# Eight routed experts after masked attention: one more expert fetched in quarter rows, and some low parts made by an adding transfer

## The chip, the cores and the metric

The kernel runs on one core of a Trainium2 chip. The metric is the device time of one execution in microseconds; runs are summed up by their median. Engines are named as the profile names them: PE multiplies matrices (PEld loads its weights), DVE is the vector engine, ACT the scalar engine, POOL is GpSimd, SP issues transfers.

## The reference

For 8 batches of 8 heads, 576 positions and 64 columns, attention scores without a softmax are multiplied by a decay `gamma ** (i - j)` under a causal mask, and by `v`. The result, laid out as 4608 tokens of 512 columns, goes to 8 experts. Routing is greedy and exact: all token and expert scores are sorted, each token goes to the best expert that still has room, and each expert takes 576 tokens.

```
logits = x @ w_gate
order = np.argsort(-logits.flatten())
...
h = np.maximum(x[mask] @ w1[e], 0.0)      # 576 x 512 by 512 x 1024
out[mask] = h @ w2[e]                     # 576 x 1024 by 1024 x 512
```

## The kernel before

**The stages.** Attention runs first, and routing is prepared beside it. Then the eight experts follow one another, in an order that routing finds while the kernel runs. They are numbered 0 to 7 here, so "the fifth expert" is number 4 and "the sixth" is number 5. Each has a first half (`l1`, products `ph`, line 1200: hidden values of 8 blocks of 128 units for two groups of token columns, s = 0 with 256 tokens and s = 1 with 320) and a second half (`l2`, products `py`, line 1348: five tiles of tokens). Numbers 6 and 7 (from `FAST` on) have another first half, `l1_fast`, line 1278.

**High and low parts.** Each float32 operand is split in two: a high part rounded for PE, and a low part, which is the value less its high part. Each product is then three matmuls: high by high, high by low, low by high. Weights arrive in the buffers `raw`; ACT makes the high part, and the low part comes either from a DVE subtraction or from a negated ACT copy of `raw` and a transfer that adds `raw` to it (`conv_lo`, line 1007, issued on POOL). The latter gives the rounded value with the opposite sign plus the value, which is the same difference. For second-half weights of experts 1, 2 and 3 the adding transfer is issued in two halves.

**Token rows.** An expert's rows are gathered from the scratch tensor `xd` by indirect transfers issued on POOL. Below `QUART` (which is 5 before) they come as whole rows: five transfers (line 1065), four PE transposes for each of five tiles (line 1154), an ACT copy for the high part (line 1156), a DVE subtraction for the low part (line 1157). From `QUART` on they come as quarter rows: 18 transfers (line 1076), a DVE transpose of 32 by 32 blocks for each of five tiles (line 1136), an ACT copy (line 1138), a DVE subtraction (line 1129), with PE taking no part. In the first half of the expert before, a quarter transfer waits behind a small POOL copy of a fresh hidden value (line 1075). The transposed rows are `xh` and `xl`. The s = 0 products read tiles 0 and 1, the s = 1 products tiles 2, 3 and 4.

**Routing beside the experts.** For the experts to come, a generator (`phases`) issues search rounds (line 351 on PE, chains of short DVE instructions around it), `members` (lines 421 and 422 on PE), `listing` (lines 459 and 462 on PE, then lines 495, 496 and 469 to 480 on DVE, which write the indices for the gathers), `leave` (lines 505 to 516) and `best` (lines 209 to 221).

**The order of instructions** is the order in which the program issues them, on each engine by itself. Where a routing step stands among the matmuls is set by a planner, `Mixer`, which adds up assumed durations in ns: `t` for PE, `v` for DVE. `adv(ns)` adds to `t` after each group of matmuls (650 for the three matmuls of one of a tile's eight blocks in `l2`, 430 in the last, smaller tile; 320 or 400 per three matmuls in `l1`). `vec(ns)` adds DVE work to `v`. When `t` reaches the time at which the planner thinks DVE is done (`v` + 150), the generator's next step is issued at that place, and its own matmuls' time is added to `t`. From expert 2 on, the DVE durations of routing are multiplied by 1.13. A tile of quarter rows is transposed at the first place where `t` has reached the due time of its last gather, 13000 after its issue; or, in the first two steps of `l1`, by force. Gathers are issued at least 1200 apart on `t`. The scatter of the results goes out on POOL, and in some experts late ones are put off to the next `l1` (`behindhand`).

At the end of `l2` the last tile `py` is moved out by an ACT copy (line 1371) and a DVE addition (line 1372). The tile's `next(tr, None)`, which issues the next piece of the following expert's transposes, stands before these two in the program; a piece that is left over is issued at the head of the following `l1`, behind them.

Of the kernel before, what the change touches and what calls it, by code (L numbers as in the profile page):

```python
# [11 lines left out]
F32 = mybir.dt.float32  # L12
F32R = mybir.dt.float32r
BF16 = mybir.dt.bfloat16
I32 = mybir.dt.int32
ALU = mybir.AluOpType
AF = mybir.ActivationFunctionType
# [3 lines left out]
NP, HP, NB = 4, 4, 9  # L21
N, DM, E, FF = 4608, 512, 8, 1024
SLACK = 1.0
QUART = 5
FAST = 6

CST = HP * 18 + 128 + 64
# [62 lines left out]
class Route:  # L90
# [337 lines left out]
    def listing(s, p):  # L428
# [45 lines left out]
        s.rows = s.idx  # L474
        if p >= QUART:
            s.rows = pool.tile([128, 20], I32, name="quart", bufs=2)
# [458 lines left out]
def moe(tc, nc, P, R, xd, w1_d, w1q_d, w2_d, out, mix):  # L935
    V, A, T = nc.vector, nc.scalar, nc.tensor
# [4 lines left out]
    state = dict(dma=0, conv=0, most=2, listing=-1, force=False)  # L941
    RAW, W1, W2, XH, XL, OPS, FEED = {}, {}, {}, {}, {}, {}, {}
# [36 lines left out]
    def free(i):  # L979
        freed.add(i)  # L980
        dma_pump()
# [16 lines left out]
    def conv_lo(by=None):  # L998

        at, raw, hi, lo = begun.pop(0)  # L1000
        e, k = divmod(at, 8)
        if by is not None:
            by.tensor_tensor(lo, raw, hi.bitcast(F32), op=ALU.subtract)
        else:
            A.activation(lo, raw, AF.Copy, scale=-1.0)
            for c in (slice(0, 512), slice(512, 1024)) if 0 < e < 4 and k >= 4 else (slice(0, 1024),):
                nc.gpsimd.dma_start(lo[:, c], raw[:, c], accum_op=ALU.add)  # L1007
        (W1 if k < 4 else W2)[e, k % 4] = (hi, lo)
        free(at)

# [45 lines left out]
    def gather(e, all=False, behind=None):  # L1056
        if e == E or not ready(e):
            return
        if e not in XG:
            xg = P["c"].tile([128, 20, 128], F32, name="xg", tag="xg")  # L1060
            XG[e] = xg
            if e < QUART:
                for j in range(5):
                    n = 128 if j < 4 else 64
                    nc.gpsimd.indirect_dma_start(out=xg[:n, 4*j:4*j+4, :].rearrange("p a c -> p (a c)"), out_offset=None, in_=xd[:, :],  # L1065
                                                 in_offset=bass.IndirectOffsetOnAxis(ap=found[e][:n, j:j+1], axis=0))
                state['arrives'] = mix.t + (9700 if e == 3 else 9000)
            else:
                LEFT[e] = list(range(18))
                state['arrives'], state['next'], state['at'] = 0, 0, {}  # L1070
        left = LEFT.get(e)
        while left and (all or mix.t >= state['next']):
            g = left.pop(0)
            if behind is not None:
                nc.gpsimd.tensor_copy(spacer4, behind.bitcast(F32))
            nc.gpsimd.indirect_dma_start(out=XG[e][:, g, :], out_offset=None, in_=xq,  # L1076
                                         in_offset=bass.IndirectOffsetOnAxis(ap=lines[e][:, g:g+1], axis=0))
            state['next'] = mix.t + 1200
            state['at'][g] = mix.t + (6000 if e >= FAST else 13000)
# [38 lines left out]
    def transposes(e):  # L1118

        if e >= FAST:  # L1120
            yield from fast_transposes(e)
            return
        xg = XG[e]
        xh = P['s'].tile([128, 4, 576], F32R, name="xh", bufs=1)
        xl = P['s'].tile([128, 4, 576], F32R, name="xl", bufs=1)
        XH[e], XL[e] = xh, xl
        if e >= QUART:
            xt = P['s'].tile([128, 4, 576], F32, name="xt", bufs=1)
            low = lambda c: V.tensor_tensor(xl[:, :, c], xt[:, :, c], xh[:, :, c].bitcast(F32), op=ALU.subtract)
            last = None  # L1130
            for j in range(5):
                n = 4 if j < 4 else 2
                while not state['force'] and state['at'].get(4*j + n - 1, mix.t + 1) > mix.t:
                    yield
                c = slice(128*j, 128*j + 32*n)
                V.transpose(xt[:, :, c].rearrange("p h (g i) -> p h g i", i=32),
                            xg[:, 4*j:4*j+n].rearrange("p g (h i) -> p h g i", h=4))
                A.activation(xh[:, :, c], xt[:, :, c], AF.Copy)
                if last is not None:
                    low(last)  # L1140
                    mix.vec(1360)
                else:
                    mix.vec(680)
                last = c
                yield
            low(last)
            mix.vec(400)
            yield
            return
        for j in range(5):  # L1150
            n = 128 if j < 4 else 64
            pt = P['bank'](("t", "h0", "h1", "h0", "h1")[j] if e else ("t", "y", "y", "t", "y")[j], [128, 4, 128], "pt", F32R)
            for d in range(4):
                T.transpose(pt[:, d, :n], xg[:n, 4*j + d].bitcast(F32R), P['ident_r'][:n, :n])  # L1154
            o, l = [x[:, :, j*128:j*128+n] for x in (xh, xl)]
            A.activation(o, pt[:, :, :n].bitcast(F32), AF.Copy)  # L1156
            V.tensor_tensor(l, pt[:, :, :n].bitcast(F32), o.bitcast(F32), op=ALU.subtract)
            mix.vec(610)
            yield
# [3 lines left out]
    def l1(e, tr):  # L1163

        hb = P['w'].tile([128, 8, 1152], F32R, name="hb", bufs=1)
        order = [(f, s) for f in (range(8) if e < QUART else (0, 4, 1, 5, 2, 6, 3, 7)) for s in range(2)]
        lows = []

        def low(ps, f, s):
            for a, b in ((0, 256),) if s == 0 else ((0, 256), (256, 320)):  # L1170
                to = (640 if a == 0 else 64) + 256*s
                V.scalar_tensor_tensor(hb[:, f, to+a:to+b], ps[:, a:b], 0.0, hb[:, f, 256*s+a:256*s+b].bitcast(F32),  # L1172
                                       op0=ALU.max, op1=ALU.subtract)
        if e == 0:
            order[1:3] = order[2], order[1]
        for i, (f, s) in enumerate(order):
            state['force'] = i < 2
            k, b = (f // 2, f % 2) if e < QUART else (f % 4, f // 4)
            wh, wl = [w.rearrange("p (f d m) -> p f d m", f=2, d=4)[:, b] for w in W1[e, k]]
            if i == 0 and e:  # L1180
                next(tr, None)
                next(tr, None)
            elif i == 1:
                for _ in tr:
                    pass
                if e == 0:
                    nc.sync.dma_start(spacer3, W1[0, 1][1][0:1, 0:1].bitcast(F32))
                    state['most'] = 8*E
                    dma_pump()
            xh, xl = XH[e], XL[e]  # L1190
            c, n = ((slice(0, 256), 256), (slice(256, 576), 320))[s]

            ps = P['bank']("y" if i // 2 in (2, 5) else f"h{s}", [128, n], "ph")
            terms = [(w[:, d], x[:, d, c]) for d in range(4) for w, x in ((wh, xh), (wh, xl), (wl, xh))]
            if (e == 0 and f < 2) or (0 < e < QUART and i == 1):
                terms = terms[0::3] + terms[2::3] + terms[1::3]
            elif e == 0 and f == 4:
                terms = terms[0::3] + terms[1::3] + terms[2::3]
            for k, (w, x) in enumerate(terms):
                T.matmul(ps, w, x, start=(k == 0), stop=(k == 11))  # L1200
                if k % 3 == 2:
                    mix.adv(320 + 80*s)
                    if e + 1 < QUART:
                        gather(e + 1)
                if k == 5 and i and e + 1 >= QUART:
                    if i % 4 != 3:
                        gather(e + 1, behind=last)
                    elif i == 7 and behindhand:
                        behindhand.pop(0)()
            A.activation(hb[:, f, c], ps, AF.Relu)  # L1210
            last = hb[0:1, f, c][:, 0:1]
            lows.append((ps, f, s))
            if i:
                low(*lows.pop(0))
            mix.vec(340 + 140*s)
            if e == 0 and i == 6:
                conv_hi()
            elif e == 0 and i == 7:
                conv_lo(V)
                mix.vec(1000)  # L1220
            if i in (2, 7, 9, 11, 13) if e == 0 else s and i // 2 in (1, 2, 3, 4):
                conv()
        owed.append(lambda: low(*lows.pop(0)))
        while behindhand:
            behindhand.pop(0)()
        return hb
# [278 lines left out]
```

## Time and profile before

| | us |
|---|---|
| median of 3 runs (605.62 to 606.1) | 605.64 |
| the profiled execution's own time | 605.43 |
| its span, first to last instruction | 603.6 |
| PE busy | 590.7 (98%) |
| DVE busy | 476.1 (79%) |
| ACT busy | 298.0 (49%) |
| POOL busy | 191.0 (32%) |

The profiled execution took 605.43 us, 1.8 more than its span, for what lies around the first and the last instruction. Matmuls are pipelined, so a busy PE is not PE at its peak; what counts is whether one matmul starts as soon as the one before allows. From the first expert on, at 160.1 us, the first halves of experts 0 to 5 take 26 to 29 us each and the second halves 25 to 31.

### The profile page before, as it was taken

The page shows a single profiled execution, that of the slowest core. Times are in us where ns is not written, and L with a number is a line of the kernel's source. Part 1 is how long each engine was busy: PE and PEld are TensorE (multiplying, and loading weights), DVE is VectorE, ACT ScalarE, POOL GpSimd, SP SyncE. Part 2 cuts the span into 40 slices and gives each one's busy share as a digit, 9 for nine tenths or more (in the row PEclk, how much of TensorE's full clock was granted, in tenths as well). Part 3 has the DMA queues.
Part 4 walks back from the last instruction along what each step waited for, and adds up shares of the span by engine and source line. Part 5 has one row for each costly group of instructions (what it writes and reads, how often), then busy time and mean ns, then how long its engine had stood idle before and what let it go on. Part 6 is the DMA issues. An engine that isn't in the chain of part 4 may idle for free.

```text
span 603.6 us, 14953 instructions
## 1 busy us (share of the span) xinstructions
PE 590.7 (98%) x5663; PEld 503.5 (83%) x5667; DVE 476.1 (79%) x1679; ACT 298.0 (49%) x649; POOL 191.0 (32%) x259
## 2 busy tenths in 40 slices
PE   9999999998999999999999999999999999999995
PEld 5887878775698889878977998799889889988973
DVE  3788989898799878987896897799985597888800
ACT  4555555542364447443662356154527357557610
POOL 0000000000511354251642362257646724861021
PEclk9999999999999999999999999999999999999998
DMA  9999999924467699795889299839876724843410
GB/s 327 401 376 334 393 351 399 351 74 150 144 194 157 206 236 243 206 228 174 184 236 257 59 226 232 233 64 241 210 207 148 211 92 107 254 147 88 114 43 35
DMA packets 51503, 125.74 MB, mean 208 GB/s; under 512 B 6352, under 2 KB 20304, under 8 KB 51432
## 3 DMA queue, kind: packets, MB, share of 16 engines
q1 hardware_dynamic: 35812, 79.77, 37.8%
q0 software_dynamic: 15296, 44.58, 32.9%
q8 instruction: 44, 0.72, 0.5%
q10 hardware_dynamic: 324, 0.45, 0.2%
q14 instruction: 27, 0.22, 0.1%
HBM read 80.21 MB, written 18.87 MB: 164 GB/s over the span
## 4 chain that ended last, share of the span: by engine, by line
PE 80%; DVE 8%; issue 6%; DMA 3%; ACT 1%; POOL 1%; POOLq 0%; SPq 0%; DVEq 0%; ACTq 0%
PE py L1348 29%; PE ph L1200 20%; PE pA L601 6%; PE pX L645 5%; PE ph L1278 4%; PE pS L624 3%; PE pX L636 2%; DMA xg<-xd,idx 2%; PE pT L683 2%; PE r L351 1%; PE warm L1443 1%; PE pt L1154 1%; DVE hb L1172 1%; PE pT L697 1%; PE r L459 1%
## 5 line engine op out<-in xcount | busy, mean ns | idle before, releaser
L1348 PE MATMUL py<-w2h,hb 128*128 128x512 f32 x576 | 186.7, 396 | 0.0
L1348 PE MATMUL py<-w2l,hb 128*128 128x512 f32 (+1 forms) x320 | 125.1, 391 | 0.0
L1348 PEld LDWEIGHTS py<-w2h,hb 128*128 128x128 f32 x576 | 104.8, 188 | 22.0
L1200 PE MATMUL ph<-xh,w1h 128*128 128x256 f32 (+1 forms) x384 | 111.2, 302 | 0.2 <-ACT xh L1156 0.2
L1200 PE MATMUL ph<-xh,w1l 128*128 128x256 f32 (+1 forms) x384 | 108.9, 296 | 0.0
L1200 PE MATMUL ph<-xl,w1h 128*128 128x256 f32 (+1 forms) x384 | 108.6, 296 | 0.0
L1065 POOL DMA_INDIRECT xg<-xd,idx x25 | 25.5, 1019 | 184.6 <-DMA raw<-in_w 152.2
L1210 ACT ACTIVATE hb<-ph 128x256 fp32r<-128x256 f32 (+1 forms) x96 | 39.1, 408 | 77.1 <-PE ph L1200 75.0
L1322 POOL DMA_INDIRECT out_y<-yt,idx x40 | 42.2, 1056 | 95.6 <-ACT yt L1369 77.2
L1200 PEld LDWEIGHTS ph<-xh,w1h 128*128 128x128 f32 x384 | 71.0, 189 | 1.3 <-ACT xh L1156 0.7
L1200 PEld LDWEIGHTS ph<-xl,w1h 128*128 128x128 f32 x384 | 71.3, 190 | 0.2
L1200 PEld LDWEIGHTS ph<-xh,w1l 128*128 128x128 f32 x384 | 71.2, 189 | 0.0
L1348 PEld LDWEIGHTS py<-w2l,hb 128*128 128x128 f32 (+1 forms) x320 | 56.7, 177 | 12.9
L1076 POOL DMA_INDIRECT xg<-xd,quart x54 | 55.4, 1026 | 15.6 <-issue 13.1
L1007 POOL DMA_DIRECT2D w2l<-raw x40 | 36.9, 1108 | 59.8 <-ACT hb L1210 47.8
L1369 ACT ACTIVATE yt<-py 128x512 f32<-128x512 f32 x32 | 19.0, 593 | 65.6 <-PE py L1348 51.3
L1172 DVE SCALAR_TENSOR_TENSOR hb<-ph,hb 128x256 fp32r<-128x256 f32 (+1 forms) x144 | 42.5, 349 | 9.7 <-ACT hb L1210 9.1
L585 ACT ACTIVATE vin<-vin,cst 128x128 f32<-128x128 f32 (+1 forms) x160 | 48.1, 379 | 1.7 <-DMA cst<-in_cst 1.7
L603 DVE TENSOR_TENSOR am<-pA,cst 128x1024 f32<-128x1024 f32 x32 | 38.9, 1214 | 12.4 <-PE pA L601 12.1
L1278 PE MATMUL ph<-xh,op 128*128 128x288 f32 x224 | 46.3, 298 | 0.2
L626 ACT ACTIVATE S<-pS 128x128 f32<-128x128 f32 x64 | 17.8, 277 | 46.0 <-PE pS L624 45.9
L601 PEld LDWEIGHTS pA<-qin,kin 64*128 64x128 f32 x512 | 31.9, 191 | 9.1 <-issue 2.9
(215 smaller groups left out, 1119.8 us busy)
## 6 DMA issues: line engine op xcount, KB each, us to landing
raw<-in_w SPq DMA_DIRECT2D x52, 512.0 KB, 5.2
w1l<-raw POOLq DMA_DIRECT2D x21, 512.0 KB, 6.9
w2l<-raw POOLq DMA_DIRECT2D x16, 512.0 KB, 5.9
kin<-in_qk SPq DMA_DIRECT2D x14, 576.0 KB, 8.0
qin<-in_qk SPq DMA_DIRECT2D x14, 576.0 KB, 6.4
vin<-in_vk SPq DMA_DIRECT2D x14, 576.0 KB, 7.7
nin<-in_vk SPq DMA_DIRECT2D x14, 512.0 KB, 8.1
xd<-xr SPq DMA_DIRECT2D x36, 192.0 KB, 6.8
```

The lines of the kernel that those rows point to most:

```text
L585: nc.scalar.activation(x, x, AF.Copy, scale=vs[:, u % HP, 4*c+h:4*c+h+1])
L601: nc.tensor.matmul(pa[:, r, j], LD[u, 'k'][half(r), s], LD[u, 'q'][half(r), s], start=True, stop=True, skip_group_check=True)
L603: nc.vector.tensor_tensor(AM[u, hf], pa, m1[:, None, None, :].to_broadcast([128, 2, 4, 128]), op=ALU.mult)
L645: nc.tensor.matmul(PX[u, hf][half(h), b, 128*c:128*c+128], v[:, a:a+64], AM[u, hf][:, h ^ b, j], start=False, stop=False, skip_group_check ...
L1007: nc.gpsimd.dma_start(lo[:, c], raw[:, c], accum_op=ALU.add)
L1076: nc.gpsimd.indirect_dma_start(out=XG[e][:, g, :], out_offset=None, in_=xq, in_offset=bass.IndirectOffsetOnAxis(ap=lines[e][:, g:g+1], axi ...
L1172: V.scalar_tensor_tensor(hb[:, f, to+a:to+b], ps[:, a:b], 0.0, hb[:, f, 256*s+a:256*s+b].bitcast(F32), op0=ALU.max, op1=ALU.subtract)
L1200: T.matmul(ps, w, x, start=(k == 0), stop=(k == 11))
L1210: A.activation(hb[:, f, c], ps, AF.Relu)
L1278: T.matmul(ps, a, x, start=(j == 0 and (late or i in (1, 2, 7))), stop=(j == 5), skip_group_check=True)
L1322: st = nc.gpsimd.indirect_dma_start(out=out[:, :], out_offset=bass.IndirectOffsetOnAxis(ap=found[e][:n, t:t+1], axis=0), in_=y[:n], in_off ...
L1348: T.matmul(ps[:m], a, w, start=(k == 0), stop=(k == last), skip_group_check=True)
```

## The change

`QUART` goes from 5 to 4, so expert 4 is now fetched in quarter rows and transposed on DVE; its weights come in the other prepared order (`w1q_d` in place of `w1_d`), and its blocks f run 0, 4, 1, 5 and so on. With `QUART` several other things move: the routing's list for expert 4 gets five more short DVE instructions (lines 478 and 480); `leave(4)` tells the planner 4700 in place of 3500; the last scatter of expert 2 is put off into the first half of expert 3; the second step of expert 4's `l1` no longer sorts its matmuls by kind (the low-row matmuls came last there).

For experts 4 and 5, the low parts of the first three row tiles are no longer DVE subtractions: ACT writes a negated copy, and an adding transfer of 256 KB is issued on POOL. A tile is transposed in parts of 64 tokens (two DVE transposes for a full tile), and `xh`, `xl` and `xt` are laid out as nine blocks of [4, 64] columns for each partition in place of [4, 576], so that a tile is contiguous and a matmul reads 4 or 5 pieces of 64. The planner is told 800 for a transposed tile and 1500 for one with the subtraction of the tile before. The adding transfers of experts 1 to 3 are issued whole. Expert 3's rows are expected 10400 ns after the gather in place of 9700.

```diff
-QUART = 5
+QUART = 4
...
             A.activation(lo, raw, AF.Copy, scale=-1.0)
-            for c in (slice(0, 512), slice(512, 1024)) if 0 < e < 4 and k >= 4 else (slice(0, 1024),):
-                nc.gpsimd.dma_start(lo[:, c], raw[:, c], accum_op=ALU.add)
+            nc.gpsimd.dma_start(lo, raw, accum_op=ALU.add)
...
-                state['arrives'] = mix.t + (9700 if e == 3 else 9000)
+                state['arrives'] = mix.t + (10400 if e == 3 else 9000)
...
+        parts = lambda x: x.rearrange("p (a h i) -> p a h i", a=9, h=4)
         if e >= QUART:
-            xt = P['s'].tile([128, 4, 576], F32, name="xt", bufs=1)
-            low = lambda c: V.tensor_tensor(xl[:, :, c], xt[:, :, c], xh[:, :, c].bitcast(F32), op=ALU.subtract)
+            XH[e], XL[e] = [lambda d, s, x=parts(x): x[:, 4*s:4+5*s, d] for x in (xh, xl)]
+            xt = P['s'].tile([128, 4*576], F32, name="xt", bufs=1)
+            low = lambda c: V.tensor_tensor(xl[:, c], xt[:, c], xh[:, c].bitcast(F32), op=ALU.subtract)
             last = None
             for j in range(5):
                 n = 4 if j < 4 else 2
                 while not state['force'] and state['at'].get(4*j + n - 1, mix.t + 1) > mix.t:
                     yield
-                c = slice(128*j, 128*j + 32*n)
-                V.transpose(xt[:, :, c].rearrange("p h (g i) -> p h g i", i=32),
-                            xg[:, 4*j:4*j+n].rearrange("p g (h i) -> p h g i", h=4))
-                A.activation(xh[:, :, c], xt[:, :, c], AF.Copy)
+                c = slice(512*j, 512*j + 128*n)
+                for a in range(2*j, 2*j + n//2):
+                    V.transpose(parts(xt)[:, a].rearrange("p h (g i) -> p h g i", i=32),
+                                xg[:, 2*a:2*a+2].rearrange("p g (h i) -> p h g i", h=4))
+                A.activation(xh[:, c], xt[:, c], AF.Copy)
+                if j < 3:
+                    A.activation(xl[:, c], xt[:, c], AF.Copy, scale=-1.0)
+                    nc.gpsimd.dma_start(xl[:, c], xt[:, c], accum_op=ALU.add)
                 if last is not None:
                     low(last)
-                    mix.vec(1360)
+                    mix.vec(1500)
                 else:
-                    mix.vec(680)
-                last = c
+                    mix.vec(800)
+                last = c if j > 2 else None
                 yield
             low(last)
             mix.vec(400)
             yield
             return
```

## Rows read from the trace of the kernel before

**Rows 1.** The page: busy us of each engine (share of the span) and instructions.

```profile
PE 590.7 (98%) x5663; PEld 503.5 (83%) x5667; DVE 476.1 (79%) x1679; ACT 298.0 (49%) x649; POOL 191.0 (32%) x259
```

**Rows 2.** PE's waits over the span: total us, times, longest us.

```profile
PE pt L1154 <- DMA xg<-xd,idx: 0.9, 3, 0.4
```

**Rows 3.** PE's timeline where expert 3's rows are transposed: start us, us, instruction.

```profile
305.97 0.61 PE L1348 MATMUL py<-w2h,hb 128*128 128x512 f32 x2
...
306.65 0.61 PE L1348 MATMUL py<-w2h,hb 128*128 128x512 f32 x2
...
307.86 0.54 PE L1154 MATMUL pt<-ident,xg 128*128 128x128 f32 x4 [0.36 <-DMA xg<-xd,idx]
...
309.01 0.46 PE L1154 MATMUL pt<-ident,xg 128*128 128x128 f32 x4
309.31 0.70 PE L1348 MATMUL py<-w2h,hb 128*128 128x512 f32 x2
...
310.08 0.45 PE L1154 MATMUL pt<-ident,xg 128*128 128x128 f32 x4
```

**Rows 4.** Second halves of experts 3 and 4: each engine's busy time (instructions), clock, DMA.

```profile
362.46:392.25 29.79, 29.79 (x182) 23.44 (x181) 22.38 (x98) 12.85 (x18) 8.01 (x12) 1.00 0.86 234
...
419.76:446.91 27.15, 27.15 (x145) 21.47 (x143) 24.75 (x99) 12.70 (x18) 14.05 (x18) 1.00 0.88 226
```

**Rows 5.** PE's timeline where expert 3's second half ends and expert 4 begins.

```profile
390.54 0.85 PE L459 MATMUL r<-rh,G 128*128 128x160 bf16 x9
391.23 0.17 PE L462 MATMUL r<-n,ones 128*128 128x8 bf16 x1
...
391.79 0.39 PE L1348 MATMUL py<-w2h,hb 128*128 128x512 f32 x1
...
392.25 0.28 PE L1200 MATMUL ph<-xh,w1h 128*128 128x256 f32 x1
```

**Rows 6.** DVE's timeline over the same place.

```profile
391.44 0.16 DVE L495 TENSOR_TENSOR room<-room,r 128x8 f32<-128x8 f32 x1 [1.45 <-PE r L462]
...
396.20 0.46 DVE L211 TENSOR_TENSOR t<-Lg,m 128x288 bf16<-128x288 f32 x1
...
397.15 0.68 DVE L1372 TENSOR_TENSOR yt<-yt,py 64x512 f32<-64x512 f32 x1
```

**Rows 7.** DVE's timeline where expert 5's last row tiles are made.

```profile
445.19 0.65 DVE L1129 TENSOR_TENSOR xl<-xt,xh 128x512 fp32r<-128x512 f32 x1
445.76 0.43 DVE L1136 STREAM_TRANSPOSE xt<-xg 128x256 f32<-128x256 f32 x1
446.12 0.99 DVE L1129 TENSOR_TENSOR xl<-xt,xh 128x512 fp32r<-128x512 f32 x2
```

**Rows 8.** ACT's timeline over the same place.

```profile
446.23 0.42 ACT L1138 ACTIVATE xh<-xt 128x256 fp32r<-128x256 f32 x1 [0.29 <-DVE xt L1136]
...
447.16 0.59 ACT L1371 ACTIVATE yt<-py 64x512 f32<-64x512 f32 x1
```

**Rows 9.** PE's timeline where expert 5's first half begins.

```profile
446.91 0.28 PE L1200 MATMUL ph<-xh,w1h 128*128 128x256 f32 x1
...
448.48 0.31 PE L1200 MATMUL ph<-xl,w1h 128*128 128x320 f32 x1
```

**Rows 10.** Transfers by line: times issued, KB each, median us to landing.

```profile
w2l<-raw POOLq DMA_DIRECT2D x24, 256.0 KB, 6.1
```

**Rows 11.** The chain that ended last, its first 12 us: start, us, what.

```profile
1.48 3.17 PE warm L1443 x7
4.65 2.01 PE pA L601 x16
6.66 0.76 PE warm L1443 x3
...
10.65 1.09 PE pA L601 x16
```

**Rows 12.** A stretch after PE's last matmul: busy time of each engine, granted clock, DMA.

```profile
597.00:603.60 6.60, 0.00 (x0) 0.00 (x0) 0.00 (x0) 0.00 (x0) 0.97 (x1) 0.77 0.10 40
```

More of the change, by code (lines that the diff above doesn't have):

```diff
@@ L1123, in transposes @@
         xg = XG[e]
-        xh = P['s'].tile([128, 4, 576], F32R, name="xh", bufs=1)
-        xl = P['s'].tile([128, 4, 576], F32R, name="xl", bufs=1)
-        XH[e], XL[e] = xh, xl
+        xh = P['s'].tile([128, 4*576], F32R, name="xh", bufs=1)
+        xl = P['s'].tile([128, 4*576], F32R, name="xl", bufs=1)
+        parts = lambda x: x.rearrange("p (a h i) -> p a h i", a=9, h=4)
         if e >= QUART:
-            xt = P['s'].tile([128, 4, 576], F32, name="xt", bufs=1)
-            low = lambda c: V.tensor_tensor(xl[:, :, c], xt[:, :, c], xh[:, :, c].bitcast(F32), op=ALU.subtract)
+            XH[e], XL[e] = [lambda d, s, x=parts(x): x[:, 4*s:4+5*s, d] for x in (xh, xl)]
+            xt = P['s'].tile([128, 4*576], F32, name="xt", bufs=1)
+            low = lambda c: V.tensor_tensor(xl[:, c], xt[:, c], xh[:, c].bitcast(F32), op=ALU.subtract)
             last = None
@@ L1149, in transposes @@
             return
+        xh, xl = [x.rearrange("p (h i) -> p h i", h=4) for x in (xh, xl)]
+        XH[e], XL[e] = [lambda d, s, x=x: x[:, d, (slice(0, 256), slice(256, 576))[s]] for x in (xh, xl)]
         for j in range(5):
@@ L1193, in l1 @@
             ps = P['bank']("y" if i // 2 in (2, 5) else f"h{s}", [128, n], "ph")
-            terms = [(w[:, d], x[:, d, c]) for d in range(4) for w, x in ((wh, xh), (wh, xl), (wl, xh))]
+            terms = [(w[:, d], x(d, s)) for d in range(4) for w, x in ((wh, xh), (wh, xl), (wl, xh))]
             if (e == 0 and f < 2) or (0 < e < QUART and i == 1):
```

## The prediction

> **What bounds the kernel now.** I read the page first. PE is busy 98% of the span [rows 1]. That alone proves little, since matmuls overlap, so I read PE's waits next: the longest total in the experts is 0.9 us, for gathered rows [rows 2]. From 160 us on PE goes from one matmul to the next. Its order of work sets the end, and a change can only gain by taking matmuls or a wait out of that order; it loses by putting a wait in. The timelines around the places that the diff touches then give the prices. DVE is the second engine to watch: in the second halves of experts 3 and 4 it works 22.4 of 29.8 us and 24.8 of 27.2 us [rows 4], mostly on routing's short instructions, each waiting for the one before.
>
> **What it removes.** Expert 4's rows no longer pass through PE: 20 transposes go from expert 3's second half. Expert 3's own transposes show what a group of four costs in place: 0.30 us from its first start to the next product (309.01 to 309.31), and the three products behind it take 0.77 us where three undisturbed ones take 0.68 (309.31 to 310.08, 305.97 to 306.65) [rows 3]. That is 0.39 us a group, and 1.9 us for five. The two second halves in the windows agree: expert 3's has the transposes, and is 2.64 us longer; about 0.7 of this is two more routing rounds of the same nine small matmuls, which leaves 1.9 [rows 4]. I take -1.9; if the products behind a group lost nothing it would be -1.5.
>
> The later arrival for expert 3: PE waited 0.36 us for the first gathered tile at 307.86 [rows 3]. On the planner's clock the first piece moves from 153,345 to 153,995, one step, so PE does three more products (0.68 us) first, and the wait goes: -0.4. If whole adding transfers, queued before these rows, landed them later, it would be 0; they carry the same bytes, so I keep -0.4.
>
> **What it adds off PE, at nothing.** 18 quarter gathers replace five, six adding transfers appear and 12 half ones go: POOL, which works 8.0 of 29.8 us there [rows 4], hides them; without that cover each would cost about a microsecond of issue. Six negated ACT copies (at the 0.6 us of a row tile's ACT copy, bound 0 to 3.8 us together) are hidden by ACT's 12.9 of 29.8 us [rows 4]. A matmul now reads pieces of 64 columns. No row shows this in float32; the nearest is routing's list matmul, which reads pieces of four bfloat16 values at 0.69 us for nine times 160 columns (390.54 to 391.23), 0.48 ns a column [rows 5], against 1.42 us for twelve times 256, 0.46, at a contiguous 256 columns (446.91 to 448.33, one product before the row at 448.48) [rows 9]. So 0 as my value, and +2% of about 52 us, 1.0 us, as the upper bound.
>
> The third row tile's adding transfer has a thin margin. It is issued at 219,755 on the planner's clock, 8.1 us before the half's end; two transposes, two ACT copies and an issue (some 3 us), and 6.1 us to land for this size [rows 10], leave about half a microsecond before the s = 1 products read it. What hides a delay there is the wait that comes next in this account; with that gone, a transfer 2 us late would cost 1 to 2 us.
>
> **What it puts in: a wait at the head of expert 4.** Here the order of instructions decides, and it follows from additions in the planner's code; these are planner ns, not device times. With the old constants they reproduce the old order: the list for expert 5 comes at 227,035, two 430-steps before the half ends at 227,895, and the trace has just two blocks of products between it and expert 4 [rows 5]. With the new ones the half runs from 201,305 to 227,895.
>
> First, gathers. The list for expert 4 is ready at 185,085, so expert 3's first half issues 8 of the 18 (three steps in four, from step 5), and the other 10 follow in the second half, every second step, from 201,955 to 214,895. The last has its due time 13,000 later, at 227,895: the last of the half's 40 steps. There the last row tile (tile 4) is transposed and tile 3's subtraction issued; tile 4's subtraction comes at the head of expert 4, behind the DVE addition that moves out the last `py`.
>
> Second, the list for expert 5. DVE's planned time stands at 221,375 when tile 2 adds 800; with `listing`'s 3700 x 1.13 that is 226,356, plus 150 is 226,506. The next step is 226,790, and 675 for its matmuls makes 227,465, one step later than before, and one step ahead of tile 4.
>
> So DVE meets, in this order: the list's tail, `leave` and the first two instructions of `best`, then tile 4's transpose, tile 3's subtraction, the addition for `py`, tile 4's subtraction. Call S the start of expert 4's first product. Before, DVE began the list's tail at 391.44, 0.81 us ahead of S = 392.25 [rows 5, 6]; with one block of products (0.46 us, 391.79 to 392.25) fewer in between it begins at S - 0.35. From there to the end of the second `best` instruction DVE took 5.22 us (391.44 to 396.66) [rows 6]: S + 4.9. The transpose takes 0.43: S + 5.3. Tile 3's subtraction, 0.65, ends at S + 5.9 [rows 7]. ACT makes tile 4's high part (0.42) by S + 5.7 and, queued behind it, moves out `py` (0.59) by S + 6.3 [rows 8]; DVE's addition (0.68) ends at S + 7.0 [rows 6]. Tile 4's subtraction is the rest of the pair at 446.12, 0.99 less 0.65 [rows 7]: S + 7.3.
>
> PE wants the low rows of all of s = 1 at its 14th product, S + 1.57 (446.91 to 448.48 at expert 5) [rows 9], and expert 4 no longer takes the low-row matmuls last in this step. PE stands for 7.3 - 1.6 = 5.7 us, with one product in the middle. What is queued behind it is the whole of expert 4. Bounds: 4.7 if the addition for `py` does not hold up the subtraction, 6.3 if DVE is half a microsecond late; 0 if the order is not as I read it.
>
> At expert 5 the same pieces come ahead of the end: the list for expert 6 moves by 1,950, DVE loses one subtraction (0.65) from its chain and gains a second transpose's 0.2, so the last subtraction, which ended 0.2 us after the start of that half (447.11) [rows 7, 9], ends 1.7 after it, against 1.57: +0.1, bounds 0 and 0.5.
>
> Sum on the profiled execution: 605.43 - 1.9 - 0.4 + 5.7 + 0.1 = 608.9. The median of the runs stands 0.2 above that execution, so 609.1 us.
>
> **The clock.** PE's granted clock was at 2.4 GHz from the first expert on. After its last matmul, at the span's end, the mean grant of 597.00 to 603.60 was 0.77 [rows 12], so it falls when PE stands. The first matmuls of the kernel show the lower level's price: sixteen took 2.01 us at 4.65, and 1.09 later, and the slow stretch went from 1.48 to 6.66 [rows 11]. The Trainium skill (TensorE: Matmul & The Clock Gate, HAM oscillation) says that a kernel whose matmuls pause for a transfer in each round falls back to the lower clock and begins each round cold; by it the wait above would be paid twice, as standing and as slow matmuls after it. No row shows a pause of this length between matmuls.
>
> **The rivals.**
> First, the wait is not there, and the kernel is faster. It needs tile 4 on DVE at least two planner steps earlier, ahead of the list's tail; it decides once the last subtraction ends before S + 1.6. For it: expert 5 before has just this tail of pieces and ends it at 447.11, ahead of need [rows 7, 9]. Against it: the order that I worked out, by one step. Then 605.43 - 1.9 - 0.4 + 0.2 = 603.3, up to 604.3 with a late adding transfer.
> Second, the clock falls in the wait. If PE needs as long to come back as at the start, 5.2 us at 1.09/2.01 of its speed, 2.4 us are lost: 611.5. For it: PE stands for some 4 us, does one product, stands again. Against it: at the end of the kernel it had been idle for longer.
> Third, the change buys a shorter wait: DVE runs ahead, or tile 4's low rows are ready early by 2 to 4 us: 605.2 to 607.2. Nothing in the rows speaks for it but the spread of DVE's waits.
>
> **How the numbers follow.** Two runs of this kernel differ by up to 0.5 us, so 0.2%, 1.2 us, is about what tells from no change. The wait at full clock has 0.50, and its own range is 607.9 (4.7 us, and 0.2 less elsewhere) to 610.0; the clock loss has 0.22 (610.5 to 612), the shorter wait 0.08, no wait 0.20 (602.5 to 604.4). The range for 8 in 10 runs from 604.0, which leaves out most of the last case, to 611.9. Slower than 606.9: the first two and half of the third, 0.76 of the chance less a little, 0.74; faster than 604.4: 0.19; between: 0.07.
>
> **What would show it.** Right: no line 1154 between 362 and 392 us; expert 3's second half some 1.9 us shorter; PE idle for 4 to 6 us at the second step of expert 4, ended by ACT's high rows and then by DVE's low rows, with DVE on lines 495 to 211 meanwhile. Wrong: PE starts that step without a gap, or is held there by the adding transfer; or a slow stretch with a grant under 1 follows. The prediction is wrong if DVE's order at S has tile 4 ahead of line 495.

## The result, and the profile after

The changed kernel takes 612.73 us, the median of five runs (611.1 to 616.02), against 605.64 before: a ratio of 1.0108, 95% interval 1.0083 to 1.0133. It is slower, as forecast, but by twice as much: 3.6 us above the 609.1 of the prediction, and 0.8 above the top of its range. The profiled execution took 611.62 us with a span of 609.8, so 6.2 us more than the profiled one of before; the working below is made against that.

The page of the changed kernel, busy time of the engines, answers to [rows 1]:

```profile
PE 591.3 (97%) x5643; PEld 503.8 (83%) x5647; DVE 477.2 (78%) x1691; ACT 301.8 (49%) x655; POOL 201.9 (33%) x274
```

Twenty PE instructions are gone, and PE is busy 0.6 us longer all the same. Its waits over the span (us in total, times, longest), against [rows 2]:

```profile
PE ph L1206 <- ACT xh L1139: 4.1, 1, 4.1
...
PE ph L1206 <- DVE xl L1129: 1.0, 1, 1.0
...
PE pt L1160 <- DMA xg<-xd,idx: 0.7, 2, 0.5
```

Two waits that were not there stand once each, on the high and then on the low rows of a quartered expert. (From the products on, line numbers are six higher than before: 1200 is 1206, 1348 is 1354, 1372 is 1378; 1136 and 1138 are 1137 and 1139.) PE's timeline at the head of expert 4, the place of [rows 5, 9]:

```profile
390.01 0.28 PE L1206 MATMUL ph<-xh,w1h 128*128 128x256 f32 x1
...
391.32 0.28 PE L1206 MATMUL ph<-xh,w1l 128*128 128x256 f32 x1
395.74 0.64 PE L1206 MATMUL ph<-xh,w1h 128*128 128x320 f32 x1 [4.13 <-ACT xh L1139]
397.40 0.64 PE L1206 MATMUL ph<-xl,w1h 128*128 128x320 f32 x1 [1.03 <-DVE xl L1129]
397.84 0.47 PE L1206 MATMUL ph<-xh,w1l 128*128 128x320 f32 x1
398.10 0.47 PE L1206 MATMUL ph<-xh,w1h 128*128 128x320 f32 x1
...
402.21 0.29 PE L1206 MATMUL ph<-xh,w1l 128*128 128x256 f32 x1
402.34 0.27 PE L1206 MATMUL ph<-xh,w1h 128*128 128x256 f32 x1
...
402.69 0.31 PE L1206 MATMUL ph<-xh,w1h 128*128 128x320 f32 x1
402.84 0.31 PE L1206 MATMUL ph<-xl,w1h 128*128 128x320 f32 x1
```

S, the start of expert 4's first product, is 390.01. Twelve products run, PE stands for 4.13 us, does one product, stands again for 1.03, and goes on with the low rows at S + 7.39. Unhindered, that product comes at S + 1.57 [rows 9]: 5.8 us are lost, standing but for the one product in between. Look then at the distances: 0.26 us between 320-column products at 398, 0.15 at 402.7. The windows give the reason (us; busy us and count of each engine; granted clock; DMA share; GB/s), first expert 3's second half, against [rows 4], then expert 4's first half and two parts of it:

```profile
361.67:390.01 28.34, 28.27 (x171) 21.90 (x170) 23.84 (x104) 14.27 (x20) 22.23 (x26) 1.00 0.93 238
390.01:424.91 34.90, 29.74 (x230) 28.89 (x228) 25.54 (x114) 14.26 (x25) 18.70 (x29) 0.90 0.65 152
395.40:402.23 6.83, 5.46 (x21) 5.12 (x22) 3.87 (x13) 1.70 (x4) 1.67 (x4) 0.50 0.19 67
402.23:424.91 22.68, 22.68 (x198) 22.39 (x197) 16.66 (x76) 12.43 (x21) 16.30 (x25) 1.00 0.73 160
```

From 395.40 to 402.23 the granted clock is 0.50, the 1.2 GHz level. The eighteen products from 397.84 to 402.21, ten of 320 columns and eight of 256, take 4.37 us; at the distances of the full clock (0.147 and 0.120) they take 2.43. With the product before them, that is some 2.2 us lost to the clock.

What DVE and ACT did meanwhile, in the order that the prediction gave (against [rows 6 to 8]). DVE's timeline:

```profile
389.65 0.16 DVE L495 TENSOR_TENSOR room<-room,r 128x8 f32<-128x8 f32 x1 [0.60 <-PE r L462]
...
394.42 0.46 DVE L211 TENSOR_TENSOR t<-Lg,m 128x288 bf16<-128x288 f32 x1
394.79 0.44 DVE L1137 STREAM_TRANSPOSE xt<-xg 128x256 f32<-128x256 f32 x1
395.15 0.65 DVE L1129 TENSOR_TENSOR xl<-xt,xh 128x512 fp32r<-128x512 f32 x1
396.33 0.68 DVE L1378 TENSOR_TENSOR yt<-yt,py 64x512 f32<-64x512 f32 x1 [0.53 <-ACT yt L1377]
396.94 0.41 DVE L1129 TENSOR_TENSOR xl<-xt,xh 128x256 fp32r<-128x256 f32 x1
```

ACT's timeline:

```profile
395.27 0.42 ACT L1139 ACTIVATE xh<-xt 128x256 fp32r<-128x256 f32 x1 [5.55 <-DVE xt L1137]
395.71 0.59 ACT L1377 ACTIVATE yt<-py 64x512 f32<-64x512 f32 x1
```

The list's tail begins at S - 0.36, tile 4's transpose at S + 4.8, its high part is done at S + 5.7, the addition for `py` at S + 7.0, tile 4's subtraction at S + 7.3. Each is within 0.2 us of the prediction's.

Where the 6.2 us of the span are, as differences of the starts of stages in the two profiled executions (us):

```
                                            before   after   change   predicted
start of expert 0's first product           160.14   160.37   +0.2
expert 2, second half (expert 3's rows)      30.53    30.07   -0.5     -0.4
expert 3, first half                         27.67    27.14   -0.5
expert 3, second half                        29.80    28.34   -1.5     -1.9
expert 4, first half                         27.51    34.90   +7.4     +5.7
expert 4, second half                        27.15    27.48   +0.3
expert 5, first half                         26.45    26.70   +0.2     +0.1
experts 5 to 7, the rest                                      +0.2
after the last product to the span's end      7.4      7.7    +0.3
```

The small differences in expert 3's first half and expert 4's second belong together with those of their neighbours: routing rounds of nine small matmuls lie in other halves now (three, four, five and two in the four halves before, two, five, four and three after, fourteen both times). So each expert's two halves are best taken together: with seven rounds both times, expert 3 takes 2.0 us less and expert 4 7.7 us more. Over experts 2 to 5 the sum is +5.5; predicted were +3.5.

The other thing to watch is the third row tile's adding transfer. The changed kernel's transfers (times, KB each, median us to landing), against [rows 10], and POOL's timeline where that transfer is issued for expert 4:

```profile
w2l<-raw POOLq DMA_DIRECT2D x28, 512.0 KB, 5.9
...
xl<-xt POOLq DMA_DIRECT2D x6, 256.0 KB, 7.0
```

```profile
385.67 1.01 POOL L1006 DMA_DIRECT2D w1l<-raw  x1
...
386.99 1.52 POOL L1328 DMA_INDIRECT out_y<-yt,idx  x1 [0.26 <-issue]
388.51 0.92 POOL L1142 DMA_DIRECT2D xl<-xt  x1
```

A row tile's 256 KB take 7.0 us to land in the median (3.6 to 8.6), about as long as the weights' 512 KB (5.9 for `w2l`, 7.8 for `w1l`), and this one stands on POOL behind a weight's transfer and a scatter. Issued at S - 1.5, it has 3.1 us to land before S + 1.57, less than the quickest of the six took. PE did not see it, since it stood until S + 7.39 in any case.

### The profile page after: what moved, and what is told of

It reads as the page before. It is cut to its first block, busy times and chain, and to the rows that moved or that the text cites. A ratio compares the mean times of both kernels' runs of the same rounds, so it can differ in the third digit from the quotient of the medians.

```text
span 609.8 us, 14948 instructions
## 1 busy us (share of the span) xinstructions
PE 591.3 (97%) x5643; PEld 503.8 (83%) x5647; DVE 477.2 (78%) x1691; ACT 301.8 (49%) x655; POOL 201.9 (33%) x274
## 4 chain that ended last, share of the span: by engine, by line
PE 79%; DVE 8%; issue 6%; DMA 2%; ACT 2%; POOL 2%; POOLq 0%; SPq 0%; DVEq 0%; ACTq 0%
PE py L1354 28%; PE ph L1206 22%; PE pA L601 6%; PE pX L645 5%; PE ph L1284 4%; PE pS L624 3%; PE pX L636 2%; PE pT L683 2%; PE r L351 2%; DVE hb L1178 1%; PE pt L1160 1%; PE pT L697 1%; PE r L459 1%; POOL xg L1064 1%; DMA raw<-in_w 1%
## 5 line engine op out<-in xcount | busy, mean ns | idle before, releaser
L1206 PE MATMUL ph<-xh,w1h 128*128 128x256 f32 (+1 forms) x384 | 112.7, 305 | 4.4 <-ACT xh L1139 4.1
L1206 PE MATMUL ph<-xl,w1h 128*128 128x256 f32 (+1 forms) x384 | 110.3, 299 | 1.0 <-DVE xl L1129 1.0
L1206 PE MATMUL ph<-xh,w1l 128*128 128x256 f32 (+1 forms) x384 | 110.3, 298 | 0.0
L1075 POOL DMA_INDIRECT xg<-xd,quart x72 | 74.7, 1037 | 21.9 <-issue 16.1
L1064 POOL DMA_INDIRECT xg<-xd,idx x20 | 20.7, 1036 | 184.8 <-DMA raw<-in_w 152.3
L1006 POOL DMA_DIRECT2D w2l<-raw x28 | 26.4, 942 | 71.6 <-ACT hb L1216 59.6
```

## The experiments

The rivals after the result. **A**: the 5.8 us come from DVE's order, the clock's fall comes with them, and nothing else of size is in the change. **B**: under that wait lies a second, the third tile's adding transfer, so that mending DVE's order gives back only a part. **C**: the standing alone costs it all, and the slow clock behind it is hidden or a matter of the record. The kernel before was timed beside every one of these runs, on the same chip, and ratios are to it. In the five sets of runs it took 605.6, 605.9, 610.5, 611.1 and 611.3 us, by chip, so times of different sets are not compared.

**Tile 4 one place earlier** (`e1_tile4_early`). Only the due time of the last two gathers of expert 4 changes, so that tile 4 comes to DVE ahead of the list's tail.

```diff
-            state['at'][g] = mix.t + (6000 if e >= FAST else 13000)
+            state['at'][g] = mix.t + (6000 if e >= FAST else 11000 if e == 4 and g > 15 else 13000)
```

> The changed kernel, with one number other: the last two quarter gathers of expert 4 count as arrived 11000 ns after issue in place of 13000 on the planner's clock, so that the last row tile (tile 4) of expert 4 stands ahead of the list's tail on DVE. First theory (the wait at the head of expert 4, 5.8 us with the slow stretch behind it 2.2 us, comes from tile 4's place in DVE's order alone): PE goes on without a gap, grant 1.0 throughout, about 603.4 us. Rival (the third row tile's low part, whose adding transfer went out at 388.5 in the changed kernel with a median of 7.0 us to land, would be awaited too, and is hidden behind the other wait): PE stands until about 395.5, some 4 us, ended by a transfer and not by DVE, and the time is about 607.3 us, more if the clock falls.

Measured: 614.38 us against 611.11, 1.0053 (1.0035 to 1.0071). PE's timeline at the head of expert 4 (S = 391.58 there), and POOL's ahead of it:

```profile
393.01 0.31 PE L1206 MATMUL ph<-xh,w1h 128*128 128x320 f32 x1
395.19 0.39 PE L1206 MATMUL ph<-xl,w1h 128*128 128x320 f32 x1 [1.87 <-DMA xl<-xt]
```

```profile
387.26 1.01 POOL L1006 DMA_DIRECT2D w1l<-raw  x1
...
388.57 1.58 POOL L1328 DMA_INDIRECT out_y<-yt,idx  x1 [0.26 <-issue]
390.14 0.93 POOL L1142 DMA_DIRECT2D xl<-xt  x1
```

The wait on DVE and ACT is gone, the first half of expert 4 falls to 28.96 us, and the wait that is left is one for the adding transfer, issued 1.4 us ahead of S. B is right, at 1.9 us; some 4 were expected from the median landing of 7.0, and here PE goes on some 5 us after the issue. This also says that DVE's order made the 5.8 us. The wait is not all of this kernel's excess over the one before: in its profile PE also stands twice in expert 5's second half, and the clock falls behind that for 3.4 us (last section).

**The wait filled** (`e2_fill_wait`, and `e2_fill_again` on another chip). PE multiplies a constant tile in the wait, 26 matmuls whose result nobody reads; the wait itself stays.

```diff
+            if e == 4 and i == 1:
+                warm(26)
             xh, xl = XH[e], XL[e]
```

> The changed kernel with 26 idle-filling matmuls of 512 columns (5.6 us at 0.216) put on PE ahead of the second step of expert 4; nothing else moves, and the wait for tile 4's low rows stays as long. First theory (the changed kernel's time is the wait plus slow matmuls after it, at the lower clock): the grant stays at 1.0, the 2.2 us of slow matmuls go, the time is about 609.4 us, and the five times lie as close together as those of the kernel before (within 0.9 us), where those of the changed kernel spread over 4.9 us. Rival (the slow matmuls and the spread come from something else, the strided reads or the transfers): the time stays at 611 to 613 us with the same spread.

Measured: 615.11 against 611.11, 1.0077 (1.0053 to 1.01). The clock stays at full from the first expert to the last product, but the time is far above the 609.4 expected, and the six runs spread over 4.1 us, not within 0.9. PE stands there for 2.25 us at once in expert 4's second half and for 1.63 in expert 5's, halves in which the kernel before stands too on another chip (last section). Without the changed kernel on the same chip the time decides little, so both ran again with the kernel before as a third.

> The kernel before, unchanged, for a profile on the same chip as the runs sent with it. On the chip of the first four runs the kernel before took 611.1 us in place of 605.6, and all four kernels had PE stand for 2 to 3 us in expert 5's second half. If that chip's transfers are slower, this profile shows PE standing there too; on a chip as the first, 605.4 to 606.1 us and no such gap.

> The changed kernel, unchanged, beside the others on one chip. A ratio of 1.008 to 1.013 to the kernel before, the wait at the head of expert 4 of 5.5 to 6 us ended by ACT and then DVE, and the lower clock after it. If the wait's length follows from DVE's order, it is the same on any chip within 0.3 us.

> The changed kernel with 26 filling matmuls in the wait, a second time, now beside the changed kernel itself. First theory (slow matmuls after the wait are a part of the loss by themselves): 2.2 us below the changed kernel run beside it, at a grant of 1.0 there. Rival: the same time as the changed kernel.

The changed kernel took 616.0 there, 1.0097 (1.0081 to 1.0112), the filled one 613.92, 1.0058 (1.0042 to 1.0073): 2.1 us less. The changed kernel's PE timeline shows the two waits of the first chip again, to 10 ns:

```profile
395.67 0.64 PE L1206 MATMUL ph<-xh,w1h 128*128 128x320 f32 x1 [4.13 <-ACT xh L1139]
397.33 0.64 PE L1206 MATMUL ph<-xl,w1h 128*128 128x320 f32 x1 [1.03 <-DVE xl L1129]
```

And the filled kernel's timeline and window of expert 4's first half:

```profile
394.27 2.97 PE L1451 MATMUL warm<-full 128*128 128x512 bf16 x13
396.89 0.50 PE L1208 MATMUL ph<-xh,w1h 128*128 128x320 f32 x1
397.41 0.41 PE L1208 MATMUL ph<-xl,w1h 128*128 128x320 f32 x1
397.66 0.30 PE L1208 MATMUL ph<-xh,w1l 128*128 128x320 f32 x1
```

```profile
390.02:422.78 32.76, 32.74 (x255) 29.12 (x254) 24.38 (x107) 14.26 (x25) 18.69 (x29) 1.00 0.71 163
```

The low rows are there at the same place, S + 7.39, and the first half of expert 4 takes 32.76 us at a grant of 1.00. The changed kernel's takes 34.90 on the first chip, and 34.15 on this one, in its window and in that of its slow stretch:

```profile
389.95:424.10 34.15, 28.99 (x230) 28.15 (x229) 24.33 (x107) 14.28 (x25) 18.67 (x29) 0.90 0.67 158
393.59:400.42 6.83, 3.72 (x12) 3.38 (x13) 4.63 (x15) 1.40 (x3) 1.27 (x2) 0.50 0.39 123
```

The waits are the same and the clock is at 0.50 for the same 6.83 us, but here from S + 3.6 on and on the first chip from S + 5.4, so that here more of the slow stretch falls into the standing. The slow clock costs 2.1 us between the medians, and 1.4 and 2.1 when the filled half is set against the two traces of the changed one. The size is uncertain to that extent; that it costs time is not, and C falls. Adding work to PE made the kernel faster.

**Tile 4 early, and one adding transfer fewer** (`e3_tile4_early_two`). As the first experiment, and the third tile of expert 4 by DVE's subtraction.

```diff
-                if j < 3:
+                if j < (2 if e == 4 else 3):
...
-                    mix.vec(1500)
+                    mix.vec(1500 if j > 3 else 800)
...
-                last = c if j > 2 else None
+                last = c if j > (1 if e == 4 else 2) else None
```

> As the run with tile 4 early, and in addition the third row tile of expert 4 gets its low part from a DVE subtraction again, with the planner told the same numbers, so that only the first two tiles use adding transfers. First theory (DVE's order alone): the same as the run with tile 4 early, about 603.4 us. Rival (the third tile's adding transfer holds PE once tile 4 is early): that run is near 607.3 and this one near 603.5 us, with no gap on PE at the head of expert 4. If both stay above 605, a third cause holds PE there.

Measured: 610.4 against 611.11, 0.9986 (0.9971 to 1.0001), on the same chip as the 1.0053 above. Expert 4's first half is 27.12 us, and PE has no wait at its head. One of the same kind has come up at expert 5, in PE's timeline:

```profile
450.12 0.38 PE L1206 MATMUL ph<-xl,w1h 128*128 128x320 f32 x1 [1.55 <-DVE sm L415]
```

The product reads `xl`; the instruction named on DVE belongs to routing and wrote nothing that it reads. The last thing that it needs is expert 5's third adding transfer, issued at 440.88, 9.2 us earlier. The trace bears this out: the weight load of this product is held by the semaphore that this transfer counts up; the last count comes at 449.98, and the hold ends at 450.01. So a second wait of B's kind stands at expert 5.

**Both experts' third tile on DVE** (`e7_second_dve`, `e7_again`). Tile 4 early; the third tile's subtraction one planner step behind its transpose, in both experts.

```diff
-                if j < 3:
+                if j < 2:
                     A.activation(xl[:, c], xt[:, c], AF.Copy, scale=-1.0)
                     nc.gpsimd.dma_start(xl[:, c], xt[:, c], accum_op=ALU.add)
+                if j == 2:
+                    yield
+                    low(c)
```

> Tile 4 early for expert 4, and for experts 4 and 5 the third row tile's low part from a DVE subtraction one planner step after its transpose; the first two tiles keep their adding transfers. If both waits are understood (DVE's order at expert 4, the third tile's adding transfer at experts 4 and 5), no gap over 0.5 us is left at the head of either expert, and 2.3 us (transposes 1.9, expert 3's rows 0.4) are gained: a ratio of 0.996, 603.3 us on a chip where the kernel before takes 605.6. If it is over 0.999, a third cost eats the gain.

> The version that beat both kernels (tile 4 of the fifth expert one place earlier; of both experts only the first two low row tiles by adding transfer), once more, on whatever chip comes, to see whether its gain is that chip's. If it is the kernel's: 0.996 to 0.999 of the kernel before. If it was chance, or that chip's: 0.999 to 1.003, as the version without any adding transfer gave.

Measured: 609.29 against 610.5 on one chip, 0.9974 (0.996 to 0.9988), and 612.05 against 611.26 on another, 1.0007 (0.999 to 1.0023). The waits at the heads of both experts are gone or under 0.4 us; a new one stands in expert 3's second half, where DVE has the third tile ahead of the list. PE's timeline in the second of the two:

```profile
390.05 0.47 PE L459 MATMUL r<-rh,G 128*128 128x160 bf16 x4 [0.99 <-DVE rh L453]
```

So the mended change is about the kernel before: one interval lies below 1, the other holds it. No version here is shown to beat it on more than one chip.

**The rest of the change alone** (`e4_rest_alone`, `e4_rest_again`): `QUART = 5`, so that expert 4's rows go through PE as before. And with it, on the same chip as the second of these, no adding transfer for rows at all, once with `QUART = 5` (`e6_rest_no_add`), once with `QUART = 4` and tile 4 early (`e8_no_add`).

```diff
-                if j < 3:
+                if j < 0:
...
-                    mix.vec(1500)
+                    mix.vec(1500 if j > 3 else 800)
...
-                last = c if j > 2 else None
+                last = c
```

> The changed kernel with the quarter threshold back at 5: expert 4 by whole rows and PE transposes as before, and all the rest of the change kept (expert 5's three low parts by adding transfers and its layout, whole adding transfers, 10400). First theory (all of the loss is expert 4's): 605.2 us, with the 0.4 us wait for expert 3's rows gone and no gap at the head of expert 5 above 0.3 us. Rival (the adding transfers or the strided reads cost something by themselves): 606 us or more, with a gap at the head of expert 5 or longer first-half products there.

> The rest of the change alone (expert 4's rows by PE as before, the sixth expert's three low row tiles by adding transfer, whole adding transfers of the weights), again, on the chip of the next two kernels, as their base. As measured before: 1.002 to 1.007 of the kernel before.

> The kernel just above, but with no adding transfer for rows: all five low row tiles of the sixth expert by DVE's subtraction. If the rows' adding transfers are what makes the rest slow (they wait on POOL and share the queues), this one stands at the kernel before, 0.998 to 1.001, and some 0.3% under the one above. If it is the other part (whole weight transfers, the step of expert 3's rows), it stays with the one above within 0.15%.

> The whole change with tile 4 of the fifth expert one place earlier, but every low row tile of both experts by DVE's subtraction, no adding transfer for rows. If the adding transfers cost more than DVE's three subtractions (2.0 us a expert, in DVE's idle time), it is the fastest: 0.994 to 0.997 of the kernel before, no wait on xl at the heads of experts 4 and 5. If DVE is the scarcer engine, its list comes late (a wait on G or r in the second half of expert 3 or 4, 1 to 2 us) and it stands at 0.998 to 1.003, above the version with two adding transfers.

Measured: 613.12 against 611.11, 1.0044 (1.002 to 1.0069), and 607.77 against 605.85, 1.0048 (1.0027 to 1.0068); without the transfers 607.67, 1.003 (1.0019 to 1.0041); with quarters and no transfers 606.09, 1.0003 (0.9989 to 1.0017). The rest is slower, and mostly not for its transfers. Nor for PE's work: in `e4_rest_again` PE's last product ends some 0.3 us later than in the first profiled execution of before, and the span is 2.0 us longer. The remainder lies behind PE's last product, in POOL's closing drain. Here it is, in the view of that line (queue, operation, times, ns shortest/median/longest, first and last start), of the kernel before (`c0_before_again`), the changed one (`c1_after_again`), the rest alone (`e4_rest_again`), and quarters without transfers (`e8_no_add`), in this order:

```profile
L1498 POOLq DRAIN  x3: 46/107/5883, 600.7 to 607.1; - x3
```

```profile
L1504 POOLq DRAIN  x3: 46/107/6158, 605.9 to 612.6; - x3
```

```profile
L1504 POOLq DRAIN  x3: 46/107/7573, 597.3 to 605.4; - x3
```

```profile
L1504 POOLq DRAIN  x3: 46/107/5910, 597.3 to 603.7; - x3
```

5.88, 6.16, 7.57 and 5.91 us, and 7.29 in `e6_rest_no_add`; where a kernel was profiled on two chips, the two agree within 10 ns. The rest alone pays 1.7 us there, the whole change 0.3. What in the program sets it these runs don't tell. A is wrong, then, in its last part: B's wait is in the change, and the rest alone costs some 2 us, most of it in a drain that the whole change does not pay. With quarters and no transfers the gain on expert 3 is there (its two halves take 1.4 us less than before), but in the profiled execution expert 6's first half takes 1.2 us more, with one wait of 0.92 us for DVE (line 1251).

## Why the prediction was wrong in size and right in kind

**The order of instructions: right.** The gathers' due time, the list one step later, tile 4 behind the list's tail, two waits with one product between: each came as worked out, and 5.8 us were measured for 5.7. Moving tile 4 alone removed it.

**The clock: the step that failed.** The prediction left it out of the sum and gave it 0.22 as the second rival. The clock fell, and cost 2.1 us between the medians of the experiment and 2.2 in the first trace, for the 2.4 that the prediction had worked out from [rows 11]. That rival's 611.5 is a median; for the profiled execution it makes 611.3, against 611.62. Of the 3.6 us between 609.1 and the measured median, 2.2 are the clock, 0.7 lie outside the stages (below), 0.9 are the median's distance from the profiled execution (1.1 us, where 0.2 was put in), and the stages give back 0.2. What spoke against the clock, that the engine "had been idle for longer" at the kernel's end, was a misreading: the 0.77 of [rows 12] is a mean, and the same stretch of the kernel before in two pieces has it so:

```profile
597.00:600.50 3.50, 0.00 (x0) 0.00 (x0) 0.00 (x0) 0.00 (x0) 0.97 (x1) 1.00 0.19 75
600.60:603.60 3.00, 0.00 (x0) 0.00 (x0) 0.00 (x0) 0.00 (x0) 0.00 (x0) 0.50 0.00 0
```

The fall came within 4.4 us of the last matmul's end (596.21), so the row did not speak against a fall in a wait of nearly six, with one product in it. In the changed kernel it came 3.8 us after the twelfth product's end (391.60), on the other chip some 2. The rule that the prediction cited, of the Trainium skill (TensorE: Matmul & The Clock Gate, HAM oscillation), spoke for the fall, and the trace agrees with it: 0.50 for 6.83 us.

**The range: the second.** Its top, 611.9, was the clock rival with little above it, because three runs of before lay within 0.5 us. Five runs of the changed kernel lie between 611.1 and 616.0, the profiled one near the low end, and the median 1.1 above it. The kernel before itself spreads over 2.6 to 4.1 us on other chips. So the spread is not the clock's alone; the filled kernel, at full clock, spread over 2.5 us, the changed one over 3.5 on that chip.

**The gains: right.** -0.5 for expert 3's row wait (-0.4 predicted; -0.3 on the chip of the filled kernel, and in `e6_rest_no_add`, with the same later arrival, PE stood there for 0.52 all the same). Expert 3's two halves lost 2.0 us together, from 57.5 to 55.5, on either chip; with `QUART = 5` and the rest of the change they take 57.7. So the 20 transposes were worth the 1.9.

**The adding transfers: right in kind, mis-sized.** "Some 3 us" up to the issue and 6.1 to land left half a microsecond. The issue came later: ACT's negated copy was done 4.5 us ahead of S, but on POOL a weight's transfer and a scatter go first, and it was issued 1.5 ahead. Landing took 7.0 in the median. Behind the mended order this costs 1.9 us, the upper end of the prediction's "1 to 2 us"; in the changed kernel it cost nothing, as said. The first rival's 603.3 left it out and its 604.3 held one microsecond of it; the kernel of that rival, tile 4 moved and nothing else, was slower than before, not faster.

**The pieces of 64 columns: nothing, as taken.** 320-column products stand 0.147 us apart at full clock, 0.46 ns a column, as the contiguous ones did.

**Left out altogether:** 0.7 us outside the stages that the change touches, 0.3 of it POOL's drain. The 0.2 ahead of expert 0 are less than executions differ by: its start lies between 159.4 and 160.8 us in those profiled.

Still open: why PE stands in some sets of runs, in all kernels, in expert 5's second half (below), which short waits bring the clock down, what sets the drain, and whether the version with two adding transfers gains anything.

## What to carry to other kernels

When a planner's constants put a short chain of work behind a longer one on the same engine, write out the order in which that engine meets its instructions; it gave the wait here to 0.1 us. A wait of several microseconds in a run of matmuls should then be priced with the slow clock in the main sum, not beside it, and what the wait covers should be listed, for removing it uncovers that. Small changes also shift costs outside every stage that they touch, so the stretch after the last product belongs into the bookkeeping.

## What the runs showed of the hardware that was not expected

**When the clock falls.** After 4.13 us of standing, one product and 1.03 more, it was at 0.50 for 6.83 us, from S + 5.4 in one execution and, with the same waits, from S + 3.6 in another. Much less can do: in the first experiment PE stood for 1.01 and 1.03 us, up to 484.45 and 485.86, and from 485.73 the clock was at 0.50 (window as above):

```profile
485.73:489.14 3.41, 3.28 (x8) 2.59 (x8) 2.19 (x5) 2.12 (x6) 1.08 (x2) 0.50 0.20 78
```

In `e4_rest_alone` waits of 0.92, 0.33 and 0.22 us, the last up to 486.00, came before a fall:

```profile
486.87:490.29 3.42, 3.42 (x10) 2.65 (x9) 3.24 (x8) 2.77 (x9) 2.32 (x4) 0.50 0.20 77
```

Yet in `e7_again` waits of 0.71, 0.34 and 0.92 us at 482.57, 483.31 and 484.73 left it at full:

```profile
484.00:490.00 6.00, 5.28 (x24) 4.54 (x25) 4.15 (x10) 3.65 (x10) 2.36 (x4) 1.00 0.16 58
```

In `e3_tile4_early_two` 1.36 and 0.35 us, up to 485.44 and 486.17, did so too. So neither the longest of such waits nor their sum tells by itself whether the clock falls.

**The same kernel on other chips.** The kernel before took 605.6 to 611.3 us. Its profile on a chip where it takes 610.5 has, beside those of the first chip, PE waits like these:

```profile
423.98 0.39 PE L351 MATMUL r<-oh,G 128*128 128x32 bf16 x9 [1.24 <-DVE G L175]
```

```profile
485.84 0.40 PE L1348 MATMUL py<-w2h,hb 128*128 128x512 f32 x1 [1.04 <-issue]
```

The second has no releaser in the records ("issue"). Gaps of this second kind stand between 482 and 492 us in the sets where the kernel before takes over 610 us, in every kernel profiled there, and not in the two where it takes under 606. Their cause is open.

**Adding transfers of one size.** 256 KB within the core took 3.6 to 8.6 us to land in one execution, and about as long as 512 KB.
